# Another order of the tokens inside a block: x in runs of 16 rows, xT read with a step of 16 elements

## The chip, the core and the metric

The program runs on one core of a Trainium2 chip. The core has five engines that run side by side: TensorE (PE, matrix products, with its own queue of weight loads), VectorE (DVE), ScalarE (ACT), GpSimd (POOL) and SyncE (SP, which here issues the transfers). PE writes its results to PSUM; everything else lies in SBUF, 128 partitions wide. Sixteen DMA engines move data between SBUF and the chip's main memory. The metric is the time of one execution on the device, in microseconds; lower is better. Before the change the median of three runs is 1611.8 us (1610.69 to 1611.89).

## The reference

Attention over a small set of points, then a two-layer network on every token. Cut to what matters here:

```
B, N, m, C = 4, 12480, 32, 128
def mab(q, kv):
    s = scale * (q @ kv.transpose(0, 2, 1))
    a = softmax(s)                      # over the last axis
    return a @ kv
h   = mab(I, x)                         # 32 points look at all tokens of a batch
out = mab(x, h)                         # each token looks at the 32 results
g   = gelu(out @ w_in)                  # 128 -> 2048
res = g @ w_out                         # 2048 -> 128
```

In `mab(I, x)` the sum over the tokens of a batch may be taken in any order. So the order in which tokens stand in the scores is free, as long as the weights and the rows of x that they multiply are in the same order.

## The kernel before

**Tiling.** The host hands in x as it is and also turned (`xT`, 128 channels by 49,920 tokens). A batch of 12,480 tokens is cut into six pieces (`sups`) of 2048 tokens, each of G = 4 blocks of 512, and a last one of two blocks of 96. A tile `xt` holds one piece of xT: 128 partitions by 2048 float32, 8 KB in each partition.

**Attention of a batch.** The first products (line 325, in `first_into`) multiply the 32 points with a piece of xT. Each block j of 512 tokens goes to 32 output partitions, 32j to 32j+31, so that four products fill one PSUM tile `pa` of 128 by 512 scores. ACT or DVE copy it to SBUF (lines 984 and 987), DVE takes the maximum (995), ACT the exponential (1061). DVE then turns each square of 32 by 32 (1081): in the result `aT`, square k of a block has its 32 tokens in the partitions and the 32 points in the columns. The weighted sums (`weigh`, line 344) multiply each square with 32 rows of x. Those come from `xn`, a tile that line 934 loads from x, once more and unturned, 32 partitions for each block, with 16 rows of 128 channels in each partition. Row i, place k of `xn` has to hold the token that stands at position 32k + i of the scores.

**Two orders.** The first batch takes its rows by turning xT on PE, and reads it by runs of 32 elements (`by_block` is true). The later three batches (`attention(b)`, b = 1 to 3) use line 323: positions in the scores are tokens in their own order, so `xn` row i, place k is token 32k + i.

**The network and the order of work.** All the time the two layers run for the tokens of earlier pieces: products with `w_in` (line 807, tile `ph`), the GELU on ACT (831 and 843), the rounded part `hi` on ACT or DVE (843, 850), the rest `lo` on DVE (859), three products with `w_out` for each of 16 chunks (886 to 888, tile `pso`), the copy out and the store (871). A planner (`Plan`) puts each job on its engine when it is built, by estimated costs: `firsts`, `gelus`, `rests` and `seconds` are the network, `attention` the next batch. In between the network's products the planner places visits, jobs that take PE for two pieces at a time: first products (line 1003 on), weighted sums (1094 on), and the second scores (line 333). A visit is reckoned by `visit` (line 950), and keeps PE from the network for its length.

**Transfers.** Everything goes through SP's queue in order: xT (line 923), x (934), the weights of the second attention (`st`, line 1290), the stores (871). `xn` has two buffers, so the load of a piece waits on SP until the weighted sums of the piece two before have read theirs.

Of the kernel before, what the change touches and what calls it, by code (L numbers as in the profile page):

```python
# [205 lines left out]
def set_attention_then_moe(ctx: ExitStack, tc, xT, x, indT, w_in, w_out, outT):  # L206
# [105 lines left out]
    def first_products(b, s, by_block):  # L312
        t0, g, w = sups[s]
        pa = ps_a.tile([P, 512], F32, tag="pa", name="pa")
        return first_into(pa, b, s, by_block)

    def first_into(pa, b, s, by_block, x=None):
        t0, g, w = sups[s]
        xg = (xts[b, s] if x is None else x)[:, 0:g * w]
        if by_block:  # L320
            xg = xg.rearrange("c (k g i) -> c g k i", g=g, i=32)
        else:
            xg = xg.rearrange("c (g t) -> c g t", g=g)
        for j in range(g):
            pe_.matmul(  # L325
                pa[32 * j:32 * j + 32, 0:w], indT_sb, xg[:, j], start=True, stop=True
            )
        return pa
# [584 lines left out]
    def since(i):  # L913
        return lambda: counts["F"] >= i
# [12 lines left out]
    def loads_x(b, units, i0):  # L927
        for s in range(NS):
            t0, g, w = sups[s]
            u = units[s]  # L930
            for j in range(g):
                def emit(u=u, t0=t0, w=w, j=j):
                    r0 = b * N + t0 + j * w
                    nc.sync.dma_start(
                        u.ap[32 * j:32 * j + 32, 0:w // 32],
                        x[r0:r0 + w, :].rearrange("(k i) c -> i k c", i=32),
                    )
                yield Job(
                    "SP", emit, 430, 6800, takes=[(r_xn, u)] if j == 0 else [], joins=[u] if j else [],
                    rank=(1, b), gate=since(i0), size=w * 512,  # L940
                )
# [11 lines left out]
    def attention(b):  # L953
# [49 lines left out]
        for v, pair in enumerate(pairs(range(NS))):  # L1003
            pas = [Unit() for _ in pair]

            def emit(pair=pair, pas=pas):
                for s, pa in zip(pair, pas):
                    first_into(pa.ap, b, s, False, x_units[b, s].ap)

            yield Job(  # L1010
                "PE", emit, visit(pair), visit(pair) + 250, [x_units[b, s] for s in pair], [],
                [(r_pa, pa) for pa in pas], rank=(0, 0), gate=since(i0 + 6 + 8 * v),
                slack=late(600, 2000),
            )
            for s, pa in zip(pair, pas):
                plan.spawn(first_out(s, pa))
# [326 lines left out]
```

## Time and profile before

| | |
|---|---|
| Median of three runs | 1611.8 us (1610.69 to 1611.89) |
| The profiled execution, on the device | 1610.68 us |
| Its span, first to last instruction | 1608.7 us |
| Mean granted clock of PE | 0.997 |
| Busy: PE, PE weight loads, DVE, ACT, POOL | 1574.9, 1227.3, 1363.5, 1317.5, 198.6 us |
| DMA: bytes, share of the 16 engines | 128.41 MB, 28.1% |

Busy shares are means over the whole span. PE's records overlap, because matmuls are pipelined: 1568 groups of three `w_out` products have a mean of about 394 ns each, but one starts every 0.23 us. So PE work is read from the starts of neighbouring records. The idle time before an instruction is put down to whatever released it last.

The first batch's attention and the decoding of the weights fill about the first 60 us. First products of the later batches stand at 86 to 131, 473 to 521 and 853 to 904 us; their weighted sums at 215 to 260, 571 to about 620 and 954 to 1001 us. From there on to the end only the network and the second scores of the last batch run.

### The profile page before, as it was taken

Reading aid. Unit: us, or ns where it says so; the run is one execution under the profiler, and the core shown is the slowest. Engines: PE = TensorE matmul, PEld = TensorE weight load, DVE = VectorE, ACT = ScalarE, POOL = GpSimd, SP = SyncE. Lnnn points to the kernel's source line nnn. Section 1 sums busy time; section 2 is a strip of 40 time slices with the busy share of each in tenths; the row PEclk is TensorE's granted clock in tenths of the full one; section 3 lists DMA queues with packets and bytes.
Section 4 is the critical chain, followed back from the end, with each engine's and each line's share of the span. In section 5 each row is a group of like instructions: output and inputs, shape, how many; then the busy total and the mean of one; then the engine's idle time right before and its main releaser. Section 6 shows DMA issues by size and latency. Waiting matters only on the chain. (4 is left out here: it accounts for less than half of the span.)

```text
span 1608.7 us, 21748 instructions
## 1 busy us (share of the span) xinstructions
PE 1574.9 (98%) x7737; PEld 1227.3 (76%) x7737; DVE 1363.5 (85%) x1518; ACT 1317.5 (82%) x1492; POOL 198.6 (12%) x134
## 2 busy tenths in 40 slices
PE   6799999999999999999999999999999999999999
PEld 3467777877887777877777777788788888788887
DVE  7799887898988888889898888798888887988886
ACT  6498888888888888878888888788888888887876
POOL 4421011020210101103010011011120110110100
PEclk9899999999999999999999999999999999999999
DMA  8371463210144193110116274301101101111100
GB/s 342 117 269 38 97 119 94 67 40 27 45 184 138 52 171 108 34 47 27 33 54 230 86 126 94 117 28 33 40 25 47 38 27 40 40 30 37 40 27 20
DMA packets 84251, 129.81 MB, mean 81 GB/s; under 512 B 12400, under 2 KB 50864, under 8 KB 78000
## 3 DMA queue, kind: packets, MB, share of 16 engines
q1 hardware_dynamic: 84144, 128.41, 28.1%
q8 instruction: 63, 1.03, 0.3%
q14 instruction: 44, 0.36, 0.1%
HBM read 74.10 MB, written 25.56 MB: 62 GB/s over the span
## 5 line engine op out<-in xcount | busy, mean ns | idle before, releaser
L859 DVE TENSOR_TENSOR lo<-g,hi 128x1024 fp32r<-128x1024 f32 (+1 forms) x784 | 983.7, 1269 | 183.1 <-ACT hi L843 172.5
L831 ACT ACTIVATE g<-ph 128x1024 f32<-128x1024 f32 (+1 forms) x784 | 804.6, 1030 | 231.4 <-PE ph L807 89.8
L886 PE MATMUL pso<-hi,wl 128*128 128x512 f32 (+1 forms) x1568 | 619.1, 395 | 0.0
L887 PE MATMUL pso<-lo,wh 128*128 128x512 f32 (+1 forms) x1568 | 616.7, 393 | 0.4 <-DVE lo L859 0.4
L888 PE MATMUL pso<-hi,wh 128*128 128x512 f32 (+1 forms) x1568 | 616.4, 393 | 0.0
L843 ACT ACTIVATE hi<-ph 128x1024 fp32r<-128x1024 f32 (+1 forms) x456 | 468.2, 1029 | 4.2 <-PE pso L888 4.0
L807 PE MATMUL ph<-st,hw 128*128 128x512 f32 x1536 | 461.5, 398 | 2.6 <-DVE hw L569 1.3
L807 PEld LDWEIGHTS ph<-st,hw 128*128 128x128 f32 x1536 | 282.8, 188 | 92.3 <-issue 10.4
L886 PEld LDWEIGHTS pso<-hi,wl 128*128 128x128 f32 x1568 | 294.3, 188 | 72.4 <-issue 3.6
L888 PEld LDWEIGHTS pso<-hi,wh 128*128 128x128 f32 x1568 | 294.1, 188 | 70.1
L887 PEld LDWEIGHTS pso<-lo,wh 128*128 128x128 f32 x1568 | 294.0, 188 | 69.4 <-DVE lo L859 0.8
L850 DVE CAST hi<-g 128x1024 fp32r<-128x1024 f32 (+1 forms) x328 | 229.6, 704 | 24.8 <-ACT g L831 16.0
L1262 POOL TENSOR_TENSOR e<-e,sm 128x512 f32<-128x512 f32 x23 | 38.7, 1682 | 1001.2 <-DVE sm L1254 792.5
L899 ACT COPY ob<-pso 128x512 f32<-128x512 f32 (+1 forms) x80 | 47.6, 595 | 13.1 <-PE pso L888 13.1
L1200 POOL TENSOR_TENSOR e<-e,m 128x512 f32<-128x512 f32 x22 | 35.0, 1601 | 87.9 <-DVE m L1194 80.2
L1264 POOL TENSOR_TENSOR e<-e,t 128x512 f32<-128x512 f32 x23 | 44.8, 1950 | 1.8
L325 PE MATMUL pa<-xt,indT_sb 128*32 128x512 f32 x192 | 25.6, 641 | 12.4 <-DMA xt<-in_xT 12.4
L1263 POOL CAST t<-e 128x512 fp32r<-128x512 f32 x23 | 32.8, 1424 | 1.5
L333 PE MATMUL pa<-xt,hT 128*32 128x512 f32 x192 | 25.5, 637 | 1.0 <-DVE hT L554 1.0
L325 PEld LDWEIGHTS pa<-xt,indT_sb 128*32 128x32 f32 x192 | 4.9, 113 | 23.5 <-issue 19.0
L344 PE MATMUL pa<-xn,t 128*32 128x128 f32 (+1 forms) x594 | 19.5, 275 | 2.9 <-DMA xn<-in_x 2.9
L344 PEld LDWEIGHTS pa<-xn,t 128*32 128x32 f32 (+1 forms) x594 | 15.5, 109 | 8.0 <-issue 5.0
(145 smaller groups left out, 464.0 us busy)
## 6 DMA issues: line engine op xcount, KB each, us to landing
xt<-in_xT SPq DMA_DIRECT2D x48, 1024.0 KB, 6.9
out_T<-ob SPq DMA_DIRECT2D x96, 256.0 KB, 2.0
st<-two SPq DMA_DIRECT2D x368, 64.0 KB, 2.0
xn<-in_x SPq DMA_DIRECT2D x72, 256.0 KB, 6.3
hw<-t SPq DMA_DIRECT2D x48, 64.0 KB, 2.5
raw<-in_w_in SPq DMA_DIRECT2D x4, 512.0 KB, 8.8
raw<-in_w_out SPq DMA_DIRECT2D x4, 512.0 KB, 8.1
st<-ahT SPq DMA_DIRECT2D x8, 64.0 KB, 2.0
```

Of the source, the lines that this page charges most:

```text
L344: pe_.matmul(pa[32 * j:32 * j + 32, 0:P], aT[0:q, kk, :], xn[0:q, kk], start=(i < G), stop=(i >= n - G),)
L807: pe_.matmul(ph[:, c, at:at + w], u.ap[:, ch % 4 * P:(ch % 4 + 1) * P], st[:, at:at + w], start=True, stop=True,)
L831: act.activation(gs[i].ap[:, :, 0:w], phs[i].ap[:, :, 0:w], AF.Gelu_apprx_sigmoid)
L843: act.activation(his[i].ap[:, :, 0:w], phs[i].ap[:, :, 0:w], AF.Gelu_apprx_sigmoid)
L850: dve.tensor_copy(his[i].ap[:, :, 0:w], gs[i].ap[:, :, 0:w])
L859: dve.tensor_sub(los[i].ap[:, :, 0:w], gs[i].ap[:, :, 0:w], his[i].ap[:, :, 0:w].bitcast(F32))
L886: pe_.matmul(o, wl[:, ch, :], hi, start=(ch == 0), stop=False)
L887: pe_.matmul(o, wh[:, ch, :], lo, start=False, stop=False)
L888: pe_.matmul(o, wh[:, ch, :], hi, start=False, stop=(ch == NCH - 1))
L899: act.copy(ob.ap[:, 0:w], pso.ap[:, 0:w])
L1262: nc.gpsimd.tensor_mul(e3, e3, sm.ap[0:q, 0:nb].unsqueeze(2).broadcast_to([q, nb, M]))
L1264: nc.gpsimd.tensor_sub(e.ap[0:q, 0:w], e.ap[0:q, 0:w], ah.ap[0:q, 0:w].bitcast(F32))
```

## The change

Two lines, both for the three later batches:

```diff
@@ first_into
         if by_block:
             xg = xg.rearrange("c (k g i) -> c g k i", g=g, i=32)
         else:
-            xg = xg.rearrange("c (g t) -> c g t", g=g)
+            xg = xg.rearrange("c (g i k) -> c g k i", g=g, i=32)
@@ loads_x
-                        x[r0:r0 + w, :].rearrange("(k i) c -> i k c", i=32),
+                        x[r0:r0 + w, :].rearrange("(i k) c -> i k c", i=32),
```

Position 32k + i of a block's scores is now token 16i + k (3i + k in the block of 96), and so is row i, place k of `xn`. A partition of `xn` now takes 16 neighbouring rows of x, 8192 bytes that lie in one piece in memory; before, it took 16 separate rows of 512 bytes, each 32 rows from the last. In return the first products read xT with a step: the inner loop over i takes every 16th float32 (64 bytes) of a partition, and the outer loop over k starts again one element further. Before, they read 512 neighbouring elements. In the blocks of 96 the step is 3 elements.

Nothing else is different. The second scores still read xT in its own order, the first batch is untouched, and no job's cost in the planner changes, so every engine has the same instructions in the same order as before. On SP only the shape of the loads differs. This is the first place, the loads of pieces 0 and 1 of batch 1; `xn` are the rows of x, `st` the weights of the second attention for the network, `ob` a finished block of the result, and the shape is partitions by elements.

```order
 L1290 DMA st_1575<-two_1573 32x512
 L871 DMA out_T<-ob_1599 128x512
-L934 DMA xn_1644<-in_x 32x16x128 x4
-L934 DMA xn_1649<-in_x 32x16x128 x4
+L934 DMA xn_1644<-in_x 32x2048 x4
+L934 DMA xn_1649<-in_x 32x2048 x4
 L1290 DMA st_1659<-two_1558 32x512
 L1290 DMA st_1659<-two_1573 32x512
```

The eight transfers stay where they were, between the same store and the same copies; each partition's 16 rows of 128 have become one run of 2048.

## The prediction

> **What bounds the kernel now.** I read the page's first two parts, then busy time by stretch, then the waits of TensorE (PE), then the timeline at the places that the change touches.
>
> ```profile
> span 1608.7 us, 21748 instructions
> PE   6799999999999999999999999999999999999999
> ...
> 440.00:540.00 100.00, 100.00 (x483) 78.75 (x483) 82.49 (x92) 81.92 (x95) 4.70 (x3) 1.00 0.39 136
> ...
> 1020.00:1600.00 580.00, 579.69 (x2534) 465.60 (x2527) 498.56 (x509) 481.45 (x527) 56.30 (x35) 1.00 0.13 37
> ```
>
> The two long rows give a stretch, its length, then busy time of PE, weight loads, DVE, ACT and POOL, the granted clock, the DMA share and GB/s. PE is busy in all of 440 to 540 us, a stretch with first products in it, at a granted clock of 1.00. DVE and ACT are free about a sixth of the time there. A busy PE is not proof of a PE at its peak, so the waits come next. These are all of PE's from 60 us on (total, times, longest):
>
> ```profile
> PE pa L344 <- DMA xn<-in_x: 2.9, 3, 1.1
> PE ph L807 <- DVE hw L569: 1.3, 1, 1.3
> PE ph L807 <- ACT hi L843: 0.9, 3, 0.3
> PE pso L887 <- DVE lo L859: 0.4, 1, 0.4
> PE ph L807 <- ACT g L831: 0.3, 2, 0.2
> ```
>
> They come to 5.8 us in some 1,550. So PE's own work sets the end: what PE has to do more, the kernel takes longer, nearly one for one. What any transfer can give back is bounded by the first row, 2.9 us; the other four rows name no transfer.
>
> **The products that change.** These rows are line 325 after the first batch, then two of its visits (a visit is two blocks of x in a row) with PE's neighbours (start, duration, engine, line, count).
>
> ```profile
> L325 PE MATMUL pa<-xt,indT_sb x144: 592/592/617, 86.5 to 891.0; 128*32 128x512 f32 x144
> L325 PE MATMUL pa<-xt_last,indT_sb x12: 246/258/270, 131.1 to 903.9; 128*32 128x96 f32 x12
> ```
>
> ```profile
> 85.95 0.39 PE L887 MATMUL pso<-lo,wh 128*128 128x512 f32 x1
> 86.18 0.40 PE L888 MATMUL pso<-hi,wh 128*128 128x512 f32 x1
> 86.51 1.92 PE L325 MATMUL pa<-xt,indT_sb 128*32 128x512 f32 x16
> 88.36 1.19 PE L807 MATMUL ph<-st,hw 128*128 128x512 f32 x4
> ...
> 889.67 1.92 PE L325 MATMUL pa<-xt,indT_sb 128*32 128x512 f32 x16
> 891.52 1.19 PE L807 MATMUL ph<-st,hw 128*128 128x512 f32 x4
> ```
>
> A visit is 16 records for eight products of the code, so each float32 product runs as two. 144 / 16 = nine visits. From the start of a visit to the start of the next work it is 88.36 - 86.51 = 1.85 us, and the same at 889.67; nine visits are 16.7 us of PE time. Sixteen records of 592 ns in 1.85 us means that several run side by side, as 32-column products into the four quarters of one tile can: four rounds of four, 0.46 us a round, 0.46 / 512 = 0.90 ns for each element of each of the four streams.
>
> The change leaves the number of instructions and their order alone. It makes each stream step 16 floats, 64 bytes, between elements, where all 512 lay in a row. What that costs PE no row shows, since no PE operand of the kernel has such a step. The nearest PE row is the first batch, whose streams jump after every 32 elements:
>
> ```profile
> 20.59 1.07 PE L325 MATMUL pa<-xt,indT_sb 128*32 128x512 f32 x8
> 21.59 1.97 PE L308 MATMUL ph<-ident,xt 128*128 128x128 f32 x16
> ```
>
> Rows of DVE and ACT by line (count, busy time, mean ns), and line 1033 by itself (least, median, most ns):
>
> ```profile
> L995 DVE TENSOR_REDUCE mx<-e 128x1 f32<-128x512 f32 x18 | 11.7, 668 | 0.2 <-ACT e L984 0.2
> L984 ACT COPY e<-pa 128x512 f32<-128x512 f32 x13 | 7.8, 619 | 0.7 <-DVE two L1272 0.7
> L618 ACT ACTIVATE sq<-raw 128x512 f32<-128x512 f32 x8 | 5.4, 681 | 2.6 <-DMA raw<-in_w_in 2.6
> ...
> L1033 DVE TENSOR_REDUCE row<-pa x3: 271/272/274, 163.5 to 938.9; 1x32 f32<-1x128 f32 x3
> ```
>
> Half a visit takes 1.00 us there, about 1.85 / 2, so a jump every 32 elements is free. On other engines, line 1033 reduces 128 floats that lie 32 floats apart in PSUM in 272 ns; line 995 reduces 512 adjacent ones in 668 ns. The difference is 396 ns for 384 elements, 1.03 ns each, so that the step costs nothing that can be seen. Line 618 reads every second word of SBUF at 681 ns for 512, against 619 ns for a plain copy on the same engine: 10% more at an 8-byte step.
>
> **Bounds and choice for the step.** From below: nothing, as on line 1033 (a gain from it I exclude: the same elements are read by the same records, and scattering them can save no fetch). From above: the streams no longer run side by side, and 16 records of 592 ns come one after another, 9.5 us a visit, +7.6 us, +69 us in all. These ends are far apart, so I ask what the port is seen to deliver. Line 888 starts 0.23 us after line 887 with 512 single-pass elements: 0.45 ns for 4 adjacent bytes. A strided float32 stream needs one element per 0.90 ns, half that rate, but with no neighbour to share a fetch. If the port fetched 8 bytes at a time, one fetch per 0.90 ns is what it does already, and the step is free. At 16 bytes a fetch comes every 4 x 0.45 = 1.8 ns, and the visit doubles. At 32 bytes it is 3.6 ns, and the visit takes four times as long. I take the doubling, the middle of the three, since line 618 shows that a step as small as 8 bytes can already cost, though on another engine: 1.85 us more for each of nine visits, +16.7 us. Not all of the 1.85 us is streaming (start and drain are in it), so this is slightly high.
>
> The Trainium skill, "SBUF — State Buffer", section "Specifications (TRN2)", speaks against the change: lines of 16 bytes, of which at least two hits are needed for full bandwidth. Here each line would be hit once; by that rule the step costs, and by its width, as an estimate, the visit would double as in the sum. No run here shows it yet, and the rule does not say that it was seen on PE.
>
> **The short block.** Its 96 columns make the step three floats, 12 bytes; the visit runs three times, 4 records each, 0.36 us long, some 1.1 us altogether. I take 0 for it, with 0 to +1 us as bounds (even doubled, it is that).
>
> **The loads of x.** 72 transfers, and 6 small ones for the short blocks, change from 16 separate rows of 512 bytes in each partition to one run of 8 KB. What their present form costs stands in three views. First the transfers by count, size and time to landing, and the packets moved from 942 to 953 us:
>
> ```profile
> xn<-in_x SPq DMA_DIRECT2D x72, 256.0 KB, 6.3
> ...
> DMA packets 3841, 1.99 MB, mean 181 GB/s; under 512 B 142, under 2 KB 3777, under 8 KB 3841
> ```
>
> The timeline of SP, DVE and PE in that place (the last batch's first two pieces):
>
> ```profile
> 942.20 6.08 SPq L934 DMA_DIRECT2D xn<-in_x  x8
> ...
> 946.51 2.83 DVE L1081 STREAM_TRANSPOSE t<-e 128x512 f32<-128x512 f32 x4 [1.63 <-ACT e L1061]
> ...
> 953.50 1.08 PE L344 MATMUL pa<-xn,t 128*32 128x128 f32 x32
> 955.64 1.08 PE L344 MATMUL pa<-xn,t 128*32 128x128 f32 x32 [1.07 <-DMA xn<-in_x]
> ```
>
> And that stretch under one in which xT, already in 8 KB runs, is loaded:
>
> ```profile
> 84.00:90.00 6.00, 6.00 (x35) 3.48 (x34) 5.93 (x9) 6.00 (x8) 3.68 (x3) 1.00 0.99 400
> 942.00:953.00 11.00, 10.69 (x46) 8.33 (x46) 7.68 (x11) 10.23 (x16) 0.00 (x0) 1.00 1.08 181
> ```
>
> The DMA engines are full in both stretches, but move 400 GB/s of the long runs and 181 GB/s of the short ones, whose packets are half a KB (1.99 MB / 3841). The two blocks' 2 MB, issued from 942.20, need over 11 us, and PE waits 1.07 us for their second half. At 400 GB/s they need 5.3 us and would be there by about 950 us, well ahead of 953.50. The DVE transposes that the same products need end at 949.3, so nothing else is late behind this wait. All three waits of line 344, 2.9 us, go. That is all: the other loads are hidden under PE work now, and stay so. SP issues stores and the `st` copies behind these loads; they get through sooner, but no wait of PE is for them. If the cover of PE work were gone, the eight-load group would cost its 5.3 us, less than the 11 now.
>
> A rule against this term is in the Trainium skill, "DMA: Bandwidth & Descriptors", section "Specifications": from 512 bytes up a transfer runs at line rate. By it the runs of 512 bytes lose nothing, the wait stays and the sum is 2.9 us higher; the trace's 181 against 400 GB/s differs from it, and decides.
>
> **ACT and DVE.** During a longer visit they get no new `ph` for another 1.85 us. They are free a sixth of the time, and PE's row for `lo`, 0.4 us in 1,550, says that the stock of finished pairs is seldom empty. I take 0 for it; were the stock short after each visit by half of that time, it would add 9 x 0.9 = 8 us.
>
> **Sum.** The profiled execution took 1610.7 us on the device for its span of 1608.7. 1610.7 + 16.7 - 2.9 = 1624.5 us. The median of the runs lies 1.1 us above the profiled one, so I forecast **1625.5 us** against 1611.8. Resolvable is about 0.2%, 3.2 us.
>
> **Rivals.**
> - *The stream keeps pace* (not slower). If PE's port delivers any word within 0.90 ns wherever it lies, the visits stay at 1.85 us and only the waits go: 1610.7 - 2.9 = 1607.8 us, or 1609 beside the median. For it: float32 products ask for elements at half the rate of line 888, and line 1033 is free of a penalty. Against it: line 618. It decides from one fetch per 0.90 ns. Its gain, 0.18%, lies at the edge of what can be told from no change. Chance 0.34.
> - *A smaller loss*: visits longer by 20 to 60%, as if some fetches were hidden: 9 x 0.37 to 1.1 less 2.9, 1612 to 1619 us. Chance 0.08.
> - *Wide fetches, or streams in each other's way*: the four streams start from places 2 KB apart and all step 64 bytes; if they meet in the same part of the memory, or a fetch is 32 bytes, the visit is three to four times 1.85: +33 to +50 us, 1642 to 1659. For it: four fetches must be served in 0.90 ns. Against it: nothing in the trace shows operands colliding. Chance 0.16.
> - *The loads do not get faster* (32 partitions at a time, where xT fills 128): the 2.9 us stay, in any of these cases. It moves each by 2.9 us and none across another.
>
> **How the numbers follow.** Doubling has 0.42, and a range of its own of 1619 to 1632 us, the top end from the late transfers, the short blocks and a little lost stock. With the smaller loss and the stream that keeps pace it is 0.84, so the range reaches from 1607 to 1632; the wide case is left out. Slower by over 0.2%: 0.42 + 0.16 + 0.05 of the smaller losses = 0.63. The case that keeps pace splits at the edge into 0.12 faster and 0.22 the same; with 0.03 of the small losses, the same is 0.25.
>
> **What would show it.** In the profile after, the time from the first record of a visit to the next work on PE decides: 1.85 us (keeps pace), 3.7 (doubling), 5.5 or more (wide). The 144 records themselves should grow from 592 ns. No wait of L344 for `xn` should be left, and the stretches with these loads should move well over 181 GB/s. If visits double but the time grows less, PE had room that I took for work; if it grows by more than nine times the visit's growth, the stock of `hi` and `lo` ran dry, and waits of L887 for DVE will say so.

## The result, and the profile after

The changed kernel takes 1624.75 us (median of 4 runs, 1624.02 to 1625.27) against 1611.83 us: a ratio of 1.0082, with a 95% interval from 1.0064 to 1.0099. It is slower by some 13 us. The forecast was 1625.5 us, in a range from 1607 to 1632.

The profiled execution took 1625.27 us, 14.6 us more than the one before (1610.68). First the records of line 325 after the first batch, by number and by least, median and most ns:

```profile
L325 PE MATMUL pa<-xt,indT_sb x144: 1043/1094/1121, 87.1 to 906.4; 128*32 128x512 f32 x144
L325 PE MATMUL pa<-xt_last,indT_sb x12: 297/301/306, 137.1 to 919.8; 128*32 128x96 f32 x12
```

Then the timeline of TensorE at the first visit, at the last visit and at the first short block (start, duration, count):

```profile
87.10 3.84 PE L325 MATMUL pa<-xt,indT_sb 128*32 128x512 f32 x16
90.87 1.19 PE L807 MATMUL ph<-st,hw 128*128 128x512 f32 x4
...
137.11 0.44 PE L325 MATMUL pa<-xt_last,indT_sb 128*32 128x96 f32 x4
137.48 0.73 PE L807 MATMUL ph<-st,hw 128*128 128x512 f32 x2
...
903.66 3.83 PE L325 MATMUL pa<-xt,indT_sb 128*32 128x512 f32 x16
907.42 1.20 PE L807 MATMUL ph<-st,hw 128*128 128x512 f32 x4
```

The median record has gone from 592 to 1094 ns, and a visit from 1.85 to 3.77 us (90.87 - 87.10; 3.76 at the last). The nine visits come to 33.95 us, against 16.7. The short block takes 0.37 us where it took 0.29. All waits of TensorE from 60 us on are now these:

```profile
PE ph L807 <- DVE hw L569: 1.2, 1, 1.2
PE ph L807 <- ACT hi L843: 0.9, 3, 0.3
PE pso L887 <- DVE lo L859: 0.4, 1, 0.4
PE ph L807 <- ACT g L831: 0.3, 2, 0.2
```

The row of line 344 for `xn`, 2.9 us before, is gone, and the other four are what they were to within 0.1 us. So the difference of the two profiles is accounted for: 17.3 us from the visits, 3 x 0.08 = 0.2 us from the short blocks, less 2.9 us, is 14.6 us.

The loads got faster, but less than forecast. The timeline of the last batch's first two pieces, and the busy time by stretch while they were loading, after the change and then before it, both from 3.8 us after the first of the eight issues on (the last two numbers are the DMA share and GB/s):

```profile
958.20 3.85 SPq L934 DMA_DIRECT2D xn<-in_x  x8
...
969.49 1.95 PE L344 MATMUL pa<-xn,t 128*32 128x128 f32 x64
```

```profile
962.00:968.00 6.00, 5.69 (x25) 4.27 (x24) 3.87 (x5) 5.97 (x12) 0.00 (x0) 1.00 1.03 219
...
946.00:952.00 6.00, 5.69 (x25) 4.27 (x24) 3.86 (x5) 5.97 (x12) 0.00 (x0) 1.00 1.22 184
```

The weighted sums run in one piece of 64 records instead of two halves. But the transfers moved 219 GB/s, a fifth more than before and not the 400 of xT, so the wait ended by little. These rows are the last of the eight transfers, its issue and its time to landing:

```profile
L934 SPq DMA_DIRECT2D xn<-in_x x1: 420/420/420, 961.6 to 961.6; - x1
...
DMA to landing us min/median/max: 8.4/8.4/8.4
```

It landed at 970.0, when the visit had begun, at 969.49. PE needs it for the second of the two pieces, half of the visit's 1.9 us later, at about 970.4. So it came some 0.4 us early. In the other two places where PE had waited, the same comparison gives 0.7 us (batch 1) and 0.2 us (batch 2).

### The profile page after: what moved, and what is told of

Same layout as the page of the kernel before. It is cut to its first block, busy times and chain, and to the rows that moved or that the text cites. A ratio compares the mean times of both kernels' runs of the same rounds, so it can differ in the third digit from the quotient of the medians.

```text
span 1623.4 us, 21748 instructions
## 1 busy us (share of the span) xinstructions
PE 1592.4 (98%) x7737; PEld 1227.9 (76%) x7737; DVE 1365.2 (84%) x1518; ACT 1319.5 (81%) x1492; POOL 196.0 (12%) x134
## 5 line engine op out<-in xcount | busy, mean ns | idle before, releaser
L325 PE MATMUL pa<-xt,indT_sb 128*32 128x512 f32 x192 | 43.2, 1019 | 12.7 <-DMA xt<-in_xT 12.7
```

Of the source, the lines that this page charges most:

```text
L325: pe_.matmul(pa[32 * j:32 * j + 32, 0:w], indT_sb, xg[:, j], start=True, stop=True)
```

## The experiments

Three questions: do the two parts of the change add up; what makes the step cost; and why did the loads stay at half of xT's speed. In all of them the kernel before is measured beside on the same chip; its median there was 1611.42, 1610.74 and 1611.22 us in the three sets.

### The step alone, and the loads alone

Each undoes one half of the change: the first keeps the new line 323, the second the new line 936.

```diff
-            xg = xg.rearrange("c (g t) -> c g t", g=g)
+            xg = xg.rearrange("c (g i k) -> c g k i", g=g, i=32)
```

> Only the first products step by 16 floats; x is loaded in runs of one row as before, so the weighted sums multiply rows in another order than the weights. If the parts simply add up: nine visits of 3.77 us for 1.85 (+17.3 us), three short blocks +0.08 us each, and the three waits of line 344 stay (2.9 us): 1611.8 + 17.5 = 1629.3 us. Rival, that the longer visits themselves give the loads the time they lack (the waits go though the loads are the old ones): 1626.4 us or less, with no wait of line 344 in the trace.

Measured: 1628.18 us, ratio 1.0104 (1.009 to 1.0118), 16.8 us more. In the profile the 144 records are the slow ones again and the waits stay:

```profile
PE pa L344 <- DMA xn<-in_x: 2.0, 2, 1.1
PE pa L344 <- DMA st<-two: 1.9, 1, 1.9
```

The second row is the same wait in batch 1, with its end put down to the copies that went through SP's queue after the loads (the last load landed at 239.48 us, PE went on at 239.62). So the rival falls: longer visits did not end the waits of line 344, which come to 3.9 us here; the new loads did.

```diff
-                        x[r0:r0 + w, :].rearrange("(k i) c -> i k c", i=32),
+                        x[r0:r0 + w, :].rearrange("(i k) c -> i k c", i=32),
```

> Only the loads of x take 8 KB runs; the first products read xT in its own order, so the weighted sums multiply rows in another order than the weights. If the loads' speed is what ends the waits: visits of 1.85 us, no wait of line 344, 1611.8 - 2.9 = 1608.9 us. Rival, that the loads moved at only about 215 GB/s after the change and met their products late enough only because the visits were longer: waits of 1 us or so remain and the time is 1610 to 1612 us.

Measured: 1607.75 us, ratio 0.9977 (0.9968 to 0.9986), 3.7 us less (2.3 to 5.2 by the interval). Its trace lists no wait of line 344, and has visits of 1.85 us. The rival falls here too: even without the longer visits the loads come in time, though by no more than 0.1 to 0.6 us in the three places. The two halves add up to 16.8 - 3.7 = 13.1 us, against 12.9 for the whole change.

### Which steps cost

```diff
-            xg = xg.rearrange("c (g t) -> c g t", g=g)
+            q = {1: 2, 2: 4, 3: 8}[b] if g == G else 1
+            xg = xg.rearrange("c (g i k) -> c g k i", g=g, k=q)
```

> The loads as before; the first products step by 2 floats in batch 1, by 4 in batch 2, by 8 in batch 3 (the weighted sums multiply rows in another order than the weights). Lines: visits of 1.85 to 1.9, 3.77 and 3.77 us, six longer ones, about 1611.8 + 11.5 = 1623 us. Hops: 3.77 us in all three, about 1629 us. Collisions (the four streams meet in one part of the memory because the step is a multiple of its parts): visits grow with the step, shorter at 4 and 8 floats than the 3.77 us at 16.

Measured: 1623.99 us, one run. The timeline of TensorE at the first visit of each batch (the added line makes 325 into 326 and 807 into 808):

```profile
87.76 2.01 PE L326 MATMUL pa<-xt,indT_sb 128*32 128x512 f32 x16
89.70 1.19 PE L808 MATMUL ph<-st,hw 128*128 128x512 f32 x4
...
475.36 3.79 PE L326 MATMUL pa<-xt,indT_sb 128*32 128x512 f32 x16
479.07 0.74 PE L808 MATMUL ph<-st,hw 128*128 128x512 f32 x2
...
860.60 3.87 PE L326 MATMUL pa<-xt,indT_sb 128*32 128x512 f32 x16
864.40 0.74 PE L808 MATMUL ph<-st,hw 128*128 128x512 f32 x2
```

1.94, 3.71 and 3.80 us. A step of 2 floats is all but free, one of 4 already costs all that one of 16 does. That is what lines of 16 bytes say: a step of 2 floats takes two words from each line, a step of 4 takes one. Hops fall (a step of 2 leaves no neighbours either), and so does a cost that grows with the step up to 16.

### Pairs, other steps, and fewer streams

The next three kernels have other orders in different batches or visits. They are read for the lengths of their visits; their times are 1621.33, 1662.97 and 1655.01 us, one run each. A stream is the operand that a product reads element by element, and four 32-column products side by side are four streams. The core of each edit:

```diff
...
+            elif b == 1:
+                xg = xg.rearrange("c (g i k p) -> c g k i p", g=g, i=32, p=2)
+            elif b == 2:
+                xg = xg.rearrange("c (g r i p) -> c g r i p", g=g, r=1, p=4)[:, :, :, :, 1:3]
+                xg = xg.broadcast_to([P, g, 2, w // 4, 2])
+            elif s < 2:
+                xg = xg.rearrange("c (g i k) -> c g k i", g=g, k=32)
+            else:
+                q = 16 if s < 4 else 1
...
+                    pe_.matmul(pa[h:h + 64, 0:w], ident[:, 0:64], xg[:, j], start=True, stop=True)
```

> Other orders of the first products, with the loads as before (part of the scores is left out or read twice, and the first pieces of the attention come out in another order than the reference's). Batch 1 reads aligned pairs of floats and jumps 64 bytes between them; batch 2 reads words 1 and 2 of each group of four, and each of them twice; batch 3 steps by 32 floats in its first visit, and in the other two runs products of 64 columns, two streams side by side, once with a step of 16 floats and once without. Lines of 16 bytes: two words of each line are enough, so 1.94 us in batches 1 and 2, as with a step of 2; 3.77 us at 32 floats; the step doubles the visit of two streams as it does with four. Rival, a port that fetches 8 aligned bytes at a time: 1.94 us in batch 1, 3.77 us in batch 2, where each word lies in a fetch of its own. Rival, collisions of four streams: more than 3.77 us at 32 floats, and with two streams the step costs much less than a doubling.

One visit of each sort, with the record that follows it (first batch 1, then 2, then the three of batch 3):

```profile
86.51 1.99 PE L340 MATMUL pa<-xt,indT_sb 128*32 128x512 f32 x16
88.43 1.19 PE L822 MATMUL ph<-st,hw 128*128 128x512 f32 x4
...
474.00 2.01 PE L340 MATMUL pa<-xt,indT_sb 128*32 128x512 f32 x16
475.94 0.73 PE L822 MATMUL ph<-st,hw 128*128 128x512 f32 x2
...
854.00 4.51 PE L340 MATMUL pa<-xt,indT_sb 128*32 128x512 f32 x16
858.45 0.73 PE L822 MATMUL ph<-st,hw 128*128 128x512 f32 x2
...
874.98 7.09 PE L337 MATMUL pa<-xt,ident 128*64 128x512 f32 x16
882.00 0.50 PE L901 MATMUL pso<-hi,wl 128*128 128x512 f32 x1
...
898.46 3.65 PE L337 MATMUL pa<-xt,ident 128*64 128x512 f32 x16
902.05 1.21 PE L822 MATMUL ph<-st,hw 128*128 128x512 f32 x4
```

Pairs that jump 64 bytes: 1.92 us. Words 1 and 2 of each line, which no aligned 8 bytes hold together: 1.94 us, so the fetch is not one of 8 aligned bytes. With two streams the step of 16 floats takes the visit from 3.59 to 7.02 us, a factor of 1.96, much as with four: the step's cost does not come from four streams meeting. But a step of 32 floats takes 4.45 us, 0.7 more than lines explain.

```diff
...
+                if b == 2:
+                    xj = xj.rearrange("c (i k) -> c k i", i=32)
+                if b < 3:
+                    pe_.matmul(pa, ident, xj, start=True, stop=True)
...
+                q = (1, 2, 16)[s // 2]
+                xj = wh[:, 4 * j:4 * j + 4].rearrange("p n c -> p (n c)").rearrange("p (i k) -> p k i", k=q)
+                pe_.matmul(pa, wh[:, 0, :], xj, start=True, stop=True)
```

> The first products are replaced by products of one stream with 128 columns, one after another (x copied by the identity, so the scores are left out): batch 1 float32 without a step, batch 2 float32 with a step of 16 floats, batch 3 single-pass (float32r) products of a weight tile with a step of 1, 2 and 16 in its three visits. Lines of 16 bytes, one per 1.8 ns and stream: float32 from about 0.43-0.46 to about 0.94 us a record, 16 records one after another, so visits of about 7 and 15 us; float32r about 0.23, 0.47 and 0.94 us a record, eight in a visit. Collisions of four streams: the step of 16 costs one stream nothing, visits of about 7 us in both batches. Rival, a fetch that is slow only because float32 takes its elements twice: float32r at a step of 2 stays at 0.23 us.

Its timeline, one visit each of batches 1 and 2 and the three of batch 3. Those three are single-pass products: their operands are float32r, 4 bytes an element too, and each product is one record where a float32 product is two:

```profile
85.84 7.03 PE L326 MATMUL pa<-xt,ident 128*128 128x512 f32 x16
92.31 1.49 PE L819 MATMUL ph<-st,hw 128*128 128x512 f32 x4
...
515.11 13.88 PE L326 MATMUL pa<-xt,ident 128*128 128x512 f32 x16
528.01 1.46 PE L819 MATMUL ph<-st,hw 128*128 128x512 f32 x2
...
901.82 2.02 PE L330 MATMUL pa<-wh 128*128 128x512 f32 x8
903.68 0.62 PE L819 MATMUL ph<-st,hw 128*128 128x512 f32 x2
...
920.00 3.78 PE L330 MATMUL pa<-wh 128*128 128x512 f32 x8
923.61 0.41 PE L898 MATMUL pso<-hi,wl 128*128 128x512 f32 x1
...
939.88 3.62 PE L330 MATMUL pa<-wh 128*128 128x512 f32 x8
943.33 1.11 PE L819 MATMUL ph<-st,hw 128*128 128x512 f32 x4
```

A single float32 stream goes from 6.47 to 12.90 us a visit, a factor of 1.99. Collisions are out as the cause at the step of 16. The single-pass products did not follow the theory: 1.86 us without a step, 3.61 with a step of 2, and 3.45, not 7.5, with one of 16. At the step of 16 they take 3.45 us / 8 / 512 = 0.84 ns for each element, and each element lies in a line of its own. So the port can take a new line every 0.84 ns, and "one line per 1.84 ns" is not its speed.

```diff
...
+                if b == 1:
+                    xj = xg[:, j * w:(j + 1) * w].rearrange("c (i k) -> c k i", k=(32, 64, 128)[v])
...
+                elif b == 2:
+                    xj = xg[:, j * w:(j + 1) * w].rearrange("c (i k) -> c k i", k=(2, 4, 32)[v])
...
+                    if v == 2:
+                        xj = xj.rearrange("p (i k t) -> p k i t", k=8, t=2)
+                    else:
+                        xj = xj.rearrange("p (i k) -> p k i", k=(4, 32)[v])
```

> More steps of the first products (the scores are left out or come in another order). Batch 1: four float32 streams with steps of 32, 64 and 128 floats in its three visits; lines alone: 3.77 us each; if a step of 32 costs more by itself, 4.45 us again and as much or more beyond. Batch 2: one float32 stream with 128 columns, steps of 2, 4 and 32 floats: 6.5, 12.9, and at 32 floats 12.9 us if what is over at 32 comes from four streams meeting, 15 us if one stream pays it alone. Batch 3: float32r with steps of 4 and 32 floats, then aligned pairs that jump 64 bytes: 3.5 us at 4 floats; pairs take 1.86 us if float32r wants both words of 8 aligned bytes, 2.7 us if every jump costs one more element's time, 3.5 us if it wants all four words of a line.

Two of its nine visits, one float32 stream at 32 floats and the single-pass pairs:

```profile
530.36 13.93 PE L328 MATMUL pa<-xt,ident 128*128 128x512 f32 x16
543.29 1.47 PE L824 MATMUL ph<-st,hw 128*128 128x512 f32 x2
...
930.70 3.62 PE L335 MATMUL pa<-wh 128*128 128x512 f32 x8
934.14 1.12 PE L824 MATMUL ph<-st,hw 128*128 128x512 f32 x4
```

From the start of a visit to the next work, in us, for all that were tried (steps in elements of 4 bytes; a visit is 16 records of float32 or 8 single-pass ones):

| step or pattern | four float32 streams | one float32 stream | one single-pass stream |
|---|---|---|---|
| 1 | 1.85 | 6.47 | 1.86 |
| 2 | 1.94 | 6.78 | 3.61 |
| pairs, 64 bytes apart | 1.92 | | 3.44 |
| words 1 and 2 of a line | 1.94 | | |
| 4 | 3.71 | 13.53 | 3.67 |
| 8 | 3.80 | | |
| 16 | 3.77 | 12.90 | 3.45 |
| 32 | 4.45 and 4.63 | 12.93 | 3.45 |
| 64 | 4.47 | | |
| 128 | 3.96 | | |

What four streams pay over 3.77 us at a step of 32, one stream alone does not pay. At 64 and 128 floats a single stream was not tried, so there it is open. For single-pass products every pattern tried but 512 neighbours takes about twice the time, and none takes more.

### Better orders

The next kernels keep rows and weights in one order, as the reference needs. Runs of 2 rows leave PE a step of 2 floats, and give the loads runs of 1 KB:

```diff
...
+            xg = xg.rearrange("c (g n i r) -> c g n r i", g=g, i=32, r=2 if g == G else 1)
...
+                        u.ap[32 * j:32 * j + 32, 0:w // 32].rearrange(
+                            "i (n r) c -> i n r c", r=2 if w == TOK else 1
+                        ),
+                        x[r0:r0 + w, :].rearrange("(n i r) c -> i n r c", i=32, r=2 if w == TOK else 1),
```

> Runs of 2 rows: the first products step by 2 floats (8 bytes), x is loaded in runs of 1 KB. Lines (PE's port takes one line of 16 bytes per 1.84 ns, and only the lines touched count): two elements from each line, 0.92 ns each, visits stay at 1.85 to 1.9 us; with the waits gone 1609 us, with the waits left 1612 us. Hops (each element that does not follow its neighbour costs the same 0.94 ns more): visits of 3.77 us, 1626 to 1629 us.

Measured: 1609.68 us, ratio 0.9991 (0.9983 to 1.0). Its trace lists no wait of line 344, and has visits of 1.94 us; the loads moved 210 GB/s:

```profile
86.57 2.01 PE L325 MATMUL pa<-xt,indT_sb 128*32 128x512 f32 x16
88.51 1.19 PE L807 MATMUL ph<-st,hw 128*128 128x512 f32 x4
```

```profile
945.00:951.00 6.00, 5.69 (x25) 4.29 (x24) 3.73 (x5) 5.97 (x12) 0.00 (x0) 1.00 1.14 210
```

That stretch, too, starts 3.7 us after the first issue. Into the same 32 partitions, rows of 512 bytes moved 184 GB/s, runs of 1 KB 210 and runs of 8 KB 219: most of what run length gives is there at 1 KB.

The sum would be 9 x 0.09 - 2.9 = -2.1 us; measured is -1.7, which the interval does not part from nothing.

The other way leaves PE out of it. The scores can stay in their own order, when the DVE transposes read them with the step (the loads are those of the change, line 323 is the old one):

```diff
-                    dve.transpose(aT[s].ap[0:q, 0:w], s1[s].ap[0:q, 0:w])
+                    dve.transpose(
+                        aT[s].ap[0:q, 0:w].rearrange("q (k m) -> q k m", m=M),
+                        s1[s].ap[0:q, 0:w].rearrange("q (i k) -> q k i", i=32),
+                    )
```

> The same order inside a block, made in another place: x is loaded in runs of 8 KB, the first products read xT without a step, and the transposes of the weights on DVE read the scores with a step of 16 floats instead. If only PE's time and the waits of line 344 count: visits of 1.85 us, no wait of line 344, the time of the loads alone, about 1608 us against 1611.4, whatever up to half a us the 18 transposes cost DVE, which is free a sixth of the time. Rival: DVE's longer transposes (700 ns now) make the weighted sums wait instead, three visits of a batch with up to 1 us each: 1611 to 1616 us.

Measured: 1607.84 us, ratio 0.9981 (0.9972 to 0.999), faster than both kernels by a margin that this measurement can tell. The transposes by line (count, busy time, mean ns), before the change and here:

```profile
L1081 DVE STREAM_TRANSPOSE t<-e 128x512 f32<-128x512 f32 x18 | 12.5, 705 | 3.3 <-ACT e L1061 3.3
...
L1081 DVE STREAM_TRANSPOSE t<-e 128x512 f32<-128x512 f32 x18 | 18.1, 1053 | 3.3 <-ACT e L1061 3.3
```

Each takes 1053 ns where it took 705, 18 x 0.35 = 6.3 us more on DVE, and the end does not see it: against the kernel before, the ratio is 0.9981 where the loads alone had 0.9977, and the two intervals overlap. The same step that costs PE 17 us costs this kernel nothing that can be told on an engine that has room.

One wait of line 344 is left, though, in batch 1:

```profile
PE pa L344 <- DMA st<-two: 1.0, 1, 1.0
```

PE went on at 233.44 us. The transposes of the batch had ended by 231.5, and the last of the visit's transfers landed at 233.3. So the load was late here and not DVE: the margin of the loads is so thin that one of three places can miss it.

### Why the loads stayed at half speed

```diff
...
+                    if j == 0:
+                        r0 = b * N + t0
+                        nc.sync.dma_start(
+                            u.ap[0:32 * g, 0:w // 32],
+                            x[r0:r0 + g * w, :].rearrange("(p k) c -> p k c", p=32 * g),
+                        )
```

> The order made on DVE as in the run before it, and each piece of x loaded by one transfer into 128 partitions instead of four into 32 each (the same 8 KB runs, and the same places in SP's queue). If the four quarter loads were held to some 215 GB/s because each fills 32 partitions only: near 400 GB/s in the loads' stretches, as for xT, and the pieces land some 4 us earlier. Rival, that reading x from memory is what is slow: some 215 GB/s again. In both cases the waits are gone already, so the time stays at that of the run before it, 0.998 of the kernel before, within 0.1%.

Measured: 1608.23 us, ratio 0.9981 (0.9971 to 0.999), the time of the run before it. The same load, by stretch, in one transfer to 128 partitions, and below it in the four transfers to 32 each of the run before it:

```profile
943.50:948.30 4.80, 4.80 (x22) 3.86 (x21) 3.17 (x4) 4.75 (x11) 0.00 (x0) 1.00 0.96 401
```

```profile
943.50:950.00 6.50, 6.24 (x27) 4.68 (x25) 4.42 (x5) 6.46 (x12) 0.00 (x0) 1.00 1.03 217
```

Same bytes, same runs of 8 KB, DMA engines full in both: 401 against 217 GB/s. So it is the shape of the transfers that held the new loads back, a quarter of the partitions and 256 KB at a time, and not memory. The run changes partitions and size together and does not tell them apart. Size alone is the less likely: from 5 to 10 us of the trace before, transfers of 0.5 and 1 MB into 128 partitions moved 411 GB/s together; none of 256 KB into 128 partitions was tried for a load. With whole pieces the last batch's first two pieces have landed by 949.1 us, 4.7 us before PE needs the second, and the trace lists no wait of line 344.

## Why the prediction was right

- *PE's own work sets the end*: right. What the visits took more is in the end nearly one for one, in the change and in the step alone.
- *Visits double*: right in the size, 3.77 us against 3.7. The term of 16.7 us measured 17.3. The remark that the term was slightly high was wrong: the time of a visit grew by more than its whole length, a factor of 2.04. The range from 1607 to 1632 us would have held a step that costs nothing, too; it is the 3.77 us that decide.
- *The reason for doubling* was half right. Fetches of 16 bytes give the right answer for float32 at every step from 2 to 16: two words of a line are enough. But the derivation, that the port delivers a line per 1.8 ns because single-pass products take 0.45 ns a word, does not hold. Single-pass products with one word in each line get a line every 0.84 ns. So why one word a line takes a float32 stream twice the time is not shown, only that it does. The doubling was also taken as the middle of three widths, which was a choice and not a deduction, and line 618, which tipped it, differs from line 984 in more than its step: it squares words from SBUF where line 984 copies from PSUM. That the size came out right is in part luck. The Trainium skill's rule ("SBUF — State Buffer", section "Specifications (TRN2)"), two hits on a line of 16 bytes for full bandwidth, agrees with all float32 rows up to a step of 16 (for four streams 1.92 to 1.94 us with two hits, 3.7 to 3.8 with one). It does not agree with the single-pass rows, where two hits cost as much as one (3.61 and 3.45 us).
- *Short block*: taken as 0, bounded by +1 us; it is 0.2 us.
- *All three waits go, 2.9 us*: right in what came of it, and shown with the loads alone and the step alone, but by luck. The step of it that was off is the transfers' speed: 400 GB/s was read from xT's loads, 1 MB into 128 partitions; these bring 256 KB into 32 and moved 219. The margin was 0.2 to 0.7 us where 3.5 had been reckoned, and in the run that makes the order on DVE the load missed it in one of the three places. The rival that named those 32 partitions was half right: the loads stayed near half of xT's speed, but the fifth that they gained was just enough to end the waits. The Trainium skill's line rate from 512 bytes up ("DMA: Bandwidth & Descriptors", section "Specifications") would have kept the wait. Here the measurement differs: into the same 32 partitions runs of 512 bytes moved 184 GB/s and runs of 8 KB 219, and the wait went with the longer ones.
- *ACT and DVE, taken as 0*: right; the rows of line 887 and of line 807 are as before, to within 0.1 us.
- *The sum*: 1624.5 us for the profiled run, which took 1625.27; the visits and the short blocks make up the 0.8 us. The 1.1 us added for the median did not come: this time the profiled run lay 0.5 us above the median. Two misses of opposite sign so brought the forecast of 1625.5 within 0.8 us of 1624.75.
- *Rivals*: the stream that keeps pace and the wide fetch are both ruled out by 3.77 us. Streams in each other's way are out as the cause at a step of 16, since one stream doubles as well; at 32 floats four streams pay 0.7 to 0.9 us a visit that one does not, which speaks for it there.

## What to carry to other kernels

Where one of two operands has to be permuted, put the step on an engine with room and keep TensorE's streams contiguous: of a float32 stream, at least two words of every 16 bytes. Count a transfer's speed from a row with the same partitions and size as well as the same run length, and look up when the last transfer landed: a wait that is gone may be gone by 0.2 us. And waits that show 2.9 us are worth about that (the loads alone gave 3.7, with 2.9 inside the interval): the faster loads could never have paid for nine visits.

## What was not expected

Single-pass products of a weight tile doubled at any pattern but neighbours, even at pairs of words (3.44 us against 1.86), and stayed there for steps of 4, 16 and 32. Four float32 streams pay 4.45 to 4.63 us at 32 floats and 4.47 at 64, more than at 16 and at 128 (3.96). Why single-pass products want neighbours where float32 is content with two words of a line, and whether and where the four streams meet, stays open: each rests on one or two visits.
